# Feature halves of 288, token sums ahead of DMA transposes, and seven block products in more places

## The chip, the cores and the metric

The kernel runs on 1 core of one Trainium2 chip. The metric is device time in microseconds of the whole launch; lower is better. Engines are named as in the profile: PE (TensorE), DVE (VectorE), ACT (ScalarE), POOL (GpSimd), SP (the queue that issues most DMAs).

## The reference

With S = 2048 tokens, D = 576 features and a hidden width of 4608, all fp32:

```python
xn = layernorm(x)                                   # over the 576 features
a = xn @ dft_hid_re.T;  b = xn @ dft_hid_im.T       # first transform, 576 -> 2 x 576
A = dft_seq_re @ a - dft_seq_im @ b                 # last stage, over the 2048 tokens
B = relu(xn @ w1) @ w2                              # 576 -> 4608 -> 576
out = x + A + B
```

## The kernel before

*Precision.* Every fp32 operand is scaled by a power of two and split into a high and a low fp16 part (`split`: ACT writes the high part, DVE the low one). A product is three fp16 matmuls: high x high, high x low, low x high, summed in PSUM.

*Seven block products.* A block matrix product of 2x2 blocks is done with 7 instead of 8 block products, with sums of blocks made beforehand (the table `PRODUCTS`, names S1..S4 for sums of the left operand, T1..T4 for those of the right one).

*Blocks.* The hidden width is cut into 9 blocks of 512. For each block b and each of 4 groups g of 512 tokens (4 tiles of 128), the first layer makes h = relu(xn @ w1), and `mlp2` makes h @ w2 by seven products, one group behind. In blocks 0 and 1 the first layer is plain: `mlp1_group` and `mlp1_step` with 512-wide matmuls. From block 2 on `pair_products` does it by seven products of 256-wide matmuls, over halves of the features and of the group's tokens. The 576 features are 4 slices of 128 and a remainder of 64 rows, so four of the products carry the remainder in two extra matmuls (`REST`). The token sums that these products need are made in block 1 by `sums_x` on DVE and ACT, out of the already transposed xT.

*Start.* A tile of 128 tokens is loaded, `stats` and `normalize` make xn and its high part, `remainder` the low part (POOL, mostly), and `transposes` turns it on PE into PSUM, from where ACT copies it into xT. Block 0's output is summed in SBUF and stored to DRAM tiles (`spill`) at its end; later blocks add to `spill` by accumulating DMAs that POOL issues.

*End.* `dft1` multiplies each token tile by the hidden transform, four column quarters of 288 each, and writes operands R. After all 16 tiles the last stage runs over 16 units (p, kh), the two kh halves of a p one after the other, each of seven products of 24 matmuls; it adds to what is read back from `spill` and stores the output.

*Order.* The order of an engine's instructions is planned at compile time from a cost model and the order of the program; the kernel steers it by lists of steps (`todo`, `work`, `brief`) and by `issue_after`. DMA loads and stores go through SP, in order; accumulating ones through POOL.

Of the kernel before, what the change touches and what calls it, by code (L numbers as in the profile page):

```python
# [18 lines left out]
P = 128  # L19
S = 2048  # L20
D = 576
# [14 lines left out]
NKX = 2 * KM + 1  # L36

NW1 = 17  # L40
W1B = NW1 * P

BB = 2
# [6 lines left out]
def kernel(  # L50
# [29 lines left out]


    dbuf = dpool.tile([P, 4 * 5 * EH], F32, name="dbuf")
    dbufs = [dbuf[:, j * 5 * EH : (j + 1) * 5 * EH] for j in range(4)]


    accs = [accp.tile([P, TG, D], F32, name=f"acc{g}") for g in range(NG)]
    acc = [accs[t // TG][:, t % TG] for t in range(NT)]
# [14 lines left out]
    def load_w1(b, i, parts=1):  # L102
        pool, tag = (raw, "raw") if b else (mlp, "stage")
        r = raws["w1", b, i] = pool.tile([P, 2 * KT, P], F32, tag=tag, name=f"raw_w1_{b}_{i}")
        n = 2 * KT // parts
        for k in range(0, 2 * KT, n):
            nc.sync.dma_start(r[:, k : k + n], w1[b, i][:, k : k + n])
# [27 lines left out]
    idle = const.tile([P, P], F16, name="idle")  # L135
# [6 lines left out]
    colno, rowno = (const.tile([P, SQ], F32, name=n) for n in ("colno", "rowno"))  # L142
# [43 lines left out]
    xT = [xpool[g].tile([P, NKX + 1, G], F16, name=f"xT{g}") for g in range(NG)]  # L186
# [49 lines left out]

    def normalize(t, eng=nc.vector):
        stage = dbufs[t % 4]
        xn = xns[t] = stage[:, :D]

        xs = xss[t] = stage[:, D : 2 * D].bitcast(F16)
        eng.tensor_scalar(xn, acc[t], means[t], factors[t], ALU.subtract, ALU.mult)
        nc.scalar.activation(xs[:, :D], acc[t], AF.Identity, bias=shifts[t], scale=factors[t])

    def remainder(t, eng):
        xn, xs = xns[t], xss[t]
        eng.tensor_tensor(
            xs[:, D : D + REM], xn[:, KM * P :], xs[:, KM * P : D], ALU.subtract
        )
        eng.tensor_tensor(  # L250
            xs[:, D + REM :], xn[:, : KM * P], xs[:, : KM * P], ALU.subtract
        )

    def transposes(t):
        xs = xss[t]
        pt = ps2.tile([P, 2, 1024], F16, tag="ps2", name=f"pt{t}")
        for k in range(NKX):
            nc.tensor.transpose(
                pt[:, k // 8, (k % 8) * P : (k % 8 + 1) * P], xs[:, k * P : (k + 1) * P], ident
            )  # L260
        g, c = divmod(t, TG)

        nc.tensor.transpose(pt[:, 1, P : 2 * P], xs[:, D - P : D], ident)
        dst = xT[g][:, :, c * P : (c + 1) * P]
        nc.scalar.activation(
            dst[:, :8, :], pt[:, 0, :].rearrange("p (k t) -> p k t", t=P), AF.Copy
        )
        nc.scalar.activation(
            dst[:, 8:, :], pt[:, 1, : 2 * P].rearrange("p (k t) -> p k t", t=P), AF.Copy
        )  # L270

# [17 lines left out]
    XK = [(kx, hl, k) for k in range(KM) for kx, hl in ((k, 0), (k, 1), (KM + 1 + k, 0))]  # L298
    XK += [(KM, 0, KM), (KM, 1, KM)]
    WK = [(kx, hl, k) for k in range(KM) for kx, hl in ((k, 1), (k, 0), (KM + 1 + k, 0))]  # L300
    WK += [(KM, 0, KM), (KM, 1, KM)]

    WK0 = sorted(WK, key=lambda w: w[1])
    w1s, w2s, us, hs = {}, {}, {}, {}
    w1bufs = [mlp.tile([P, W1B], F32, name=f"w1buf{i}", bufs=1) for i in range(2)]
    w1bufs += [dbuf[:, i * W1B : (i + 1) * W1B] for i in range(2)]

    def mlp1_group(b, g, i, cols, ps, wk=WK, start=True, stop=True):
        for n, (kx, hl, k) in enumerate(wk):
            nc.tensor.matmul(  # L310
                ps[:, cols], w1s[b, i // 2][:, hl, i % 2 * KT + k], xT[g][:, kx, cols],
                start=(start and n == 0), stop=(stop and n == len(wk) - 1),
            )

    def new_ps1(b, g, i):
        return ps1.tile([P, G], F32, tag="ps1", name=f"p1_{b}_{g}_{i}")

    def mlp1(b, g, i):
        ps = new_ps1(b, g, i)
        mlp1_group(b, g, i, slice(0, G), ps)  # L320
        return ps

    def mlp1_step(b, g, i, ps):

        if i == 1:
            for j in range(NF):  # L330
                r, kx = j % 2, (KM, NKX)[j % 2]
                rows = slice(r * REM, (r + 1) * REM)
                if j:
                    ps.append(new_ps1(b, g, j))
                nc.tensor.matmul(
                    ps[j], w1s[b, j // 2][rows, 1, r * KT + KM], xT[g][rows, kx],
                    start=(j > 0), stop=(j == 0),
                )
        if i == 0:
            ps.append(new_ps1(b, g, 0))  # L340
        mlp1_group(b, g, i, slice(0, G), ps[i], WK[:-1], start=(i == 0), stop=(i > 0))

    def mlp1_out(b, g, i, pa, pb):
# [24 lines left out]
    LEFT = (0, 2, 8, 15, 13, 10, 5)  # L368
    REST = {P2: (4, 0), P5: (7, 1), P3: (12, 1), P4: (7, 0)}
    flat = [a.rearrange("p a b -> p (a b)") for a in accs]  # L370
    XS = 4 * 2 * (KM // 2) * GH // 2
    xsums = [
        f[:, : XS].bitcast(F16).rearrange("p (q n k t) -> p q n k t", q=4, n=2, t=GH)
        for f in flat
    ]
    cbufs = [f[:, XS :] for f in flat]
    H1, H2 = slice(0, GH), slice(GH, G)

    def halves(g, q):

        r, c = q
        k, t = 2 * r, (H1, H2)[c]
        return xT[g][:, k : k + 2, t], xT[g][:, KM + 1 + k : KM + 3 + k, t]

    def right(g, n):
        if n in (P1, P2, P3):
            return halves(g, {P1: (0, 0), P2: (1, 0), P3: (1, 1)}[n])
        x = xsums[g][:, {P5: 0, P6: 1, P4: 2, P7: 3}[n]]
        return x[:, 0], x[:, 1]

    def sums_x(g):


        f = [
            w[:, 2 * KT * P :][:, : 2 * GH].rearrange("p (k t) -> p k t", t=GH) for w in w1bufs[2:]
        ]
        tt = nc.vector.tensor_tensor
        for q, (head, tail) in enumerate((
            ((0, 1), (0, 0)), ((1, 1), None), ((1, 0), None), ((1, 1), (0, 1)),
        )):  # L400
            t = f[q % 2]
            h, l = halves(g, head)
            if tail:
                h2, l2 = halves(g, tail)
                tt(t, h, h2, ALU.subtract)
                tt(t, t, l2, ALU.subtract)
            else:
                tt(t, h, f[1 - q % 2], ALU.subtract)
            tt(t, t, l, ALU.add)
            yield  # L410
            hi, lo = (xsums[g][:, q, n] for n in range(2))
            nc.scalar.activation(hi, t, AF.Copy)
            yield
            tt(lo, t, hi, ALU.subtract)  # L414
# [7 lines left out]
    def pair_products(b, g, i):  # L422
# [10 lines left out]
        def product(n):  # L433
# [3 lines left out]
            todo = [  # L437
                (ws[:, y, a + k], x[z][:, k]) for k in range(2) for y, z in ((1, 0), (0, 0), (0, 1))
            ]
            if n in REST:  # L440
                k, c = REST[n]
                todo += [(ws[:, y, k], xT[g][:, KM, (H1, H2)[c]]) for y in range(2)]
# [51 lines left out]
    sumbufs = [mlp.tile([P, 2, EH], F32, name="sum0", bufs=1)] + [  # L494
        dbuf[:, k : k + 2 * EH].rearrange("p (c e) -> p c e", e=EH)
        for k in (2 * W1B, 2 * W1B + 2 * EH)
# [10 lines left out]
    def mlp2(b, g, n):  # L507
# [18 lines left out]
        blocks = accs[g].rearrange("p (h c) (j e) -> p h j c e", h=2, j=2)  # L526
        o = sums[row, col] = sums[row, col] if b else blocks[:, row, col]
        if b and n in (0, 2, 3, 6):
# [5 lines left out]
        if b and n not in (0, 2, 3):  # L534
            nc.gpsimd.dma_start(spill[g, row, col], o, accum_op=ALU.add)  # L535
        if b == 0 and n == 6:
            for r in range(2):
                for j in range(2):
                    nc.sync.dma_start(spill[g, r, j], blocks[:, r, j])
# [3 lines left out]
    def max_w1(b, f):  # L543
# [6 lines left out]
        with tc.issue_after(order["vfree"]) if b >= BB else nullcontext():  # L550
            magnitude(mx["f", b][:, r : r + 1], raws["w1", b, i][:, r * KT : (r + 1) * KT])
        if r:
            if b >= BB:
# [10 lines left out]
    def power_w1(b, i):  # L564
        s, p = (t["w1", b][:, i : i + 1] for t in (sc, pw))
        if b >= BB:
# [3 lines left out]

    def split_w1(b, f):
        i, r = divmod(f, 2)
        k = slice(r * KT, (r + 1) * KT)
        if r == 0:
            w = w1bufs[b % 2 * 2 + i].bitcast(F16)[:, : 4 * KT * P]
            w1s[b, i] = w.rearrange("p (n k f) -> p n k f", n=2, f=P)
        w = w1s[b, i]
        split(w[:, 0, k], w[:, 1, k], raws["w1", b, i][:, k], sc["w1", b][:, i : i + 1])

    def split_w1b(b, i, c):  # L580

        if c == 0:
            w = w1bufs[b % 2 * 2 + i].bitcast(F16)
            w1s[b, i] = w.rearrange("p (n k f) -> p n k f", n=2, f=P)
        w, r = w1s[b, i], raws["w1", b, i]
        src = (r[:, :5], r[:, 7:], r[:, :5], r[:, 5:9])[c]
        k = (slice(0, 5), slice(5, 8), slice(8, 13), slice(13, 17))[c]
        split(w[:, 0, k], w[:, 1, k], src, sc["w1", b][:, i : i + 1])

    def sums_w1(b, i):  # L590
        r = raws["w1", b, i]
# [632 lines left out]
```

## Time and profile before

| | |
|---|---|
| median of 2 runs | 1266.02 us (1264.86 to 1267.18) |
| span of the profiled execution | 1265.5 us; its page gives no other time |
| PE, DVE, ACT, POOL busy | 1242.4, 1024.9, 706.8, 148.9 us |
| mean granted PE clock | 0.995 |
| block 0 and 1 | 0 to 213 us |
| blocks 2 to 8 | 213 to 823 us |
| first transform | 823 to 929 us |
| last stage | 929 to 1262 us |

The boundaries are first and last starts of the matmul lines (310, 444, 1037, 1156). Busy time counts overlapping parts of an engine's pipeline once; the pace of matmuls is read from their starts.

### The profile page before, as it was taken

How to read it: one execution, taken by the hardware profiler on the slowest of the kernel's cores; microseconds unless marked ns; L12 is line 12 of the kernel's file. 1: busy time of each engine (PE TensorE's matmuls, PEld its weight loads, DVE VectorE, ACT ScalarE, POOL GpSimd, SP SyncE). 2: the span in 40 equal slices, each digit the busy share in tenths (PEclk: the TensorE clock that was granted, in tenths of full speed). 3: DMA queues.
4: the chain of work that ended last, by engine and by line, in shares of the span. 5: the costliest groups of instructions: out<-in, count | busy, mean ns of one | idle time of the engine just before them, and what ended most of it. 6: DMA issues, size and time to landing. Idle time of an engine off the chain costs nothing.

```text
span 1265.5 us, 25525 instructions
## 1 busy us (share of the span) xinstructions
PE 1242.4 (98%) x10396; PEld 991.3 (78%) x10396; DVE 1024.9 (81%) x1933; ACT 706.8 (56%) x1194; POOL 148.9 (12%) x188
## 2 busy tenths in 40 slices
PE   8899999999999999999999999999999999999998
PEld 7665566888888888888888888877777777777776
DVE  8899999778878787788798878556788888787875
ACT  5835466666676676676766766544453333333332
POOL 2320021121212121212121212100000000000000
PEclk8999999999999999999999999999999999999999
DMA  6022357666657676666666666630053434434320
GB/s 246 23 78 85 112 128 149 125 134 140 131 120 154 139 142 123 128 154 113 133 144 147 137 138 124 114 94 1 1 171 100 147 122 145 141 111 144 117 86 20
DMA packets 60806, 150.75 MB, mean 119 GB/s; under 512 B 6288, under 2 KB 21136, under 8 KB 60688
## 3 DMA queue, kind: packets, MB, share of 16 engines
q1 hardware_dynamic: 42256, 111.36, 26.8%
q0 software_dynamic: 18432, 37.76, 22.0%
q8 instruction: 81, 1.33, 0.4%
q14 instruction: 37, 0.30, 0.1%
HBM read 101.91 MB, written 47.19 MB: 118 GB/s over the span
## 4 chain that ended last, share of the span: by engine, by line
PE 79%; DVE 13%; ACT 3%; issue 2%; DMA 2%; SPq 0%; POOL 0%; ACTq 0%; DVEq 0%
PE p L521 24%; PE bank L444 23%; PE p L1156 22%; PE pd L1037 8%; DVE cs L183 1%; PE p L310 1%; DVE w2s L183 1%; DVE acc L532 1%; DMA raw_w<-in_w_dram 1%; DVE h L354 1%; DVE w1buf L183 1%; DVE acc L414 1%; DVE st L200 1%; DVE h L361 1%; DMA c<-in_cim_dram 1%
## 5 line engine op out<-in xcount | busy, mean ns | idle before, releaser
L521 PE MATMUL p<-w2s,h 128*128 128x288 f16 x3024 | 408.7, 286 | 3.1 <-DVE h L466 1.5
L521 PEld LDWEIGHTS <-h 128*128 128x128 f16 x3024 | 295.4, 98 | 78.2 <-issue 2.3
L1156 PE MATMUL p<-R,cs 128*128 128x288 f16 x2688 | 329.8, 286 | 2.5 <-DVE o L1162 2.5
L1156 PEld LDWEIGHTS <-cs 128*128 128x128 f16 x2688 | 263.0, 98 | 69.1 <-issue 2.9
L182 ACT ACTIVATE cs<-c,sc_c 128x1024 f16<-128x1024 f32 x112 | 128.0, 1147 | 195.0 <-PE p L1156 135.0
L183 DVE SCALAR_TENSOR_TENSOR cs<-c,sc_c,cs 128x1024 f16<-128x1024 f32 x112 | 143.4, 1283 | 40.6 <-ACT cs L182 40.5
L444 PEld LDWEIGHTS <-w1buf 128*128 128x128 f16 x1600 | 156.5, 98 | 23.0 <-issue 1.6
L444 PEld LDWEIGHTS <-dbuf 128*128 128x128 f16 x1200 | 117.4, 98 | 16.1
L444 PE MATMUL bank<-xT,w1buf 128*128 128x256 f16 x832 | 109.9, 273 | 0.0
L1037 PE MATMUL pd<-dbuf,xT 128*128 128x288 f16 x832 | 103.8, 286 | 0.0
L444 PE MATMUL bank<-acc,w1buf 128*128 128x256 f16 x768 | 102.1, 273 | 1.4 <-ACT acc L470 1.4
L1037 PEld LDWEIGHTS <-xT 128*128 128x128 f16 x832 | 80.8, 98 | 22.0 <-issue 1.9
L466 DVE TENSOR_TENSOR h<-s,h 128x1024 f16<-128x1024 f32 x56 | 68.5, 1224 | 33.9 <-ACT h L463 33.6
L451 ACT ACTIVATE h<-acc 128x256 f16<-128x256 f32 x112 | 46.0, 411 | 76.4 <-DVE acc L474 71.1
L535 POOL DMA_DIRECT2D spill<-dbuf x70 | 61.0, 876 | 232.9 <-DVE dbuf L532 194.2
L444 PE MATMUL bank<-xT,dbuf 128*128 128x256 f16 x624 | 82.5, 273 | 0.0
L463 ACT ACTIVATE h<-s 128x1024 f16<-128x1024 f32 x56 | 59.1, 1056 | 37.0 <-DVE s L458 36.4
L444 PE MATMUL bank<-acc,dbuf 128*128 128x256 f16 x576 | 76.6, 273 | 0.0
L1162 DVE SCALAR_TENSOR_TENSOR o<-p,us_c,o 128x288 f32<-128x288 f32 x112 | 57.5, 514 | 19.2 <-PE p L1156 19.1
L911 ACT ACTIVATE f<-f 128x1024 f32<-128x1024 f32 x64 | 66.9, 1046 | 0.8 <-DMA f<-in_cre_dram 0.8
L452 DVE SCALAR_TENSOR_TENSOR h<-acc,h 128x256 f16<-128x256 f32 x112 | 47.3, 422 | 21.1 <-ACT h L451 21.0
L530 ACT ACTIVATE dbuf<-p,c_ub 128x576 f32<-128x576 f32 x70 | 51.0, 730 | 15.3 <-PE p L521 15.0
(156 smaller groups left out, 1556.1 us busy)
## 6 DMA issues: line engine op xcount, KB each, us to landing
spill<-dbuf POOLq DMA_DIRECT2D x70, 288.0 KB, 5.3
f<-in_cre_dram SPq DMA_DIRECT2D x32, 512.0 KB, 5.9
f<-in_cim_dram SPq DMA_DIRECT2D x32, 512.0 KB, 5.6
c<-in_cre_dram SPq DMA_DIRECT2D x32, 512.0 KB, 4.2
c<-in_cim_dram SPq DMA_DIRECT2D x32, 512.0 KB, 4.7
spill<-sum POOLq DMA_DIRECT2D x42, 288.0 KB, 4.6
raw_w<-in_w_dram SPq DMA_DIRECT2D x17, 640.0 KB, 6.4
raw_w<-in_w_dram SPq DMA_DIRECT2D x18, 576.0 KB, 4.9
```

The costliest lines, as they stand in the source:

```text
L182: nc.scalar.activation(hi, src, AF.Copy, scale=s)
L183: nc.vector.scalar_tensor_tensor(lo, src, s, hi, ALU.mult, ALU.subtract)
L444: nc.tensor.matmul(ps, l, r, start=first and m == 0, stop=m == len(todo) - 1, skip_group_check=not first,)
L463: order["s"] = nc.scalar.activation(hi_s, st[:, 1:], AF.Copy).ins
L466: order["lo"] = nc.vector.tensor_tensor(lo_s, st[:, 1:], hi_s, ALU.subtract).ins
L521: nc.tensor.matmul(ps[:, c], h[:, x, qa, c * P : (c + 1) * P], w[:, y, qb], start=first and i == 0 and j == 0, stop=i == NQ - 1 and j == 2 ...
L530: freed(nc.scalar.activation(o, ps, AF.Copy, scale=us[b]))
L535: nc.gpsimd.dma_start(spill[g, row, col], o, accum_op=ALU.add)
L911: nc.scalar.activation(f, f, AF.Abs, scale=2.0**-10, accum_out=sums_c[:, n, q : q + 1])
L1037: nc.tensor.matmul(ps[j], xT[g][:, kx, c * P : (c + 1) * P], dsp[j][:, hl, k], start=(t % 2 == 0 and n == 0), stop=(t % 2 == 1 and n == le ...
L1156: nc.tensor.matmul(ps, w[:, a, k], r[:, c, rq], start=first and k == 0 and j == 0, stop=k == HK - 1 and j == 2, skip_group_check=not first,)
L1162: order["o"] = nc.vector.scalar_tensor_tensor(o, ps, us["c"][:, n : n + 1], o, ALU.mult, ALU.add).ins
```

## The change

*Feature halves.* The 576 features become two halves of 288, each with two slices of 128 and one packed slice: 32 remainder rows as high, high, low and zero. A half then needs 7 matmuls (`PASSES`): three for each full slice and one for the packed one. `load_w1` brings the remainder rows by broadcast DMAs (`load_rest`), `high`, `low` and `split_operands` build the packed slices.

*Transposes.* Tiles 0 to 3 stay on PE; tiles 4 to 15 are transposed by DMA from SP, SBUF to SBUF. The stages of the normalized tiles go from 4 to 7, and xn stays in the tile's own place.

*Token sums.* `sums_x` runs in block 0, on POOL, over the untransposed xn (four subtractions of blocks, each in two parts), splits the sums (ACT and POOL) and transposes them by DMA.

*Block 1* is done by `pair_products` too. Block 0 no longer sums in SBUF: `copy_x` copies x into `spill` from DRAM to DRAM, and block 0 adds to it like the others.

*First transform.* `dft1` is replaced by chains of seven products, over feature halves, token halves and column halves; the right sums of R are made afterwards on POOL or DVE. Half of its weights (`dsp[1]`) is prepared after block 8's first layer, in the place of block 8's weights.

*Last stage.* The order becomes: transform of token half 0, its 8 units (their results added to `spill` by POOL's DMAs), transform of half 1, its 8 units. Four of seven evictions per unit of half 0 go to ACT.

```diff
-    XK = [(kx, hl, k) for k in range(KM) for kx, hl in ((k, 0), (k, 1), (KM + 1 + k, 0))]
-    XK += [(KM, 0, KM), (KM, 1, KM)]
+    PASSES = [p for k in range(2) for p in ((3 + k, k), (k, k), (k, 3 + k))] + [(2, 2)]
...
     def transposes(t):
+        if t >= TG:
+            nc.sync.dma_start_transpose(dst, xs)
+            return
...
+    def load_rest(dst, src):
+        shape = list(src.shape)
+        nc.sync.dma_start(dst, src.unsqueeze(0).to_broadcast([P // RH] + shape))
...
     def sums_x(g):
+        b11, b21, b12, b22 = (half(pair(c), r) for c in range(2) for r in range(2))
+        for dst, a, b in ((b11, b12, b11), (b12, b22, b12), (b22, b22, b11), (b21, b21, b22)):
+            for k in range(2):
+                nc.gpsimd.tensor_tensor(dst[k], a[k], b[k], ALU.subtract)
+            yield
+        for c in range(TG):
+            st = spare[:, c % 2]
+            high(st, xns[t])
+            low(st, xns[t], nc.gpsimd)
+            if c < 2:
+                nc.sync.dma_start_transpose(s0[:, :, cols], st.rearrange("p r k c -> p (r k c)"))
+            else:
+                for r, dst in ((1, s1[:, :, cols]), (0, xT[g][:, :KC, GH:][:, :, cols])):
+                    nc.sync.dma_start_transpose(dst, st[:, r].rearrange("p k c -> p (k c)"))
+            yield
...
     def mlp2(b, g, n):
-        if b and n in (0, 2, 3, 6):
+        if n in (0, 2, 3, 6):
...
-        if b >= BB:
+        if b:
             first, second = (pair_products(b, g, i) for i in range(NQ))
...
+    load_later = prepare_d(1)
     for q in range(7):
         mlp2(*steps[-1], q)
+        for _ in range(2):
+            if load_later:
+                load_later.pop(0)()
...
+    def chain(g, c, z):
+        u, v, w = (bank(f"pd{t}_{z}_{k}") for k in range(3))
+        copy = lambda o, p: nc.scalar.activation(o, p, AF.Copy, scale=HALF)
+        add = lambda o, p: stt(o, p, HALF, o, ALU.mult, ALU.add)
+        def product(n):
+            ps = {P2: v, P5: w, P3: w}.get(n, u)
+            for m, (y, k) in enumerate(PASSES):
+                nc.tensor.matmul(ps, x[:, k, c * P : (c + 1) * P], dsp[z][:, a, y], ...)
+    def transform(kh, at):
+        for n, key in enumerate(keys + [None]):
+            for f, q in ((new, P1), (old, P7), (new, P2), (old, P3), (new, P6), (old, P4), (new, P5)):
...
+    transform(0, side)
+    for n in range(HK):
+        unit(n)
+    transform(1, side2)
+    for n in range(HK, 2 * HK):
+        unit(n)
```

More of the change, by code (lines that the diff above doesn't have):

```diff
@@ L79 @@
     ps2 = tc.alloc_tile_pool(name="ps2", bufs=2, space=PSUM)
[L82 to L87, printed above, removed]
+    dbuf = dpool.tile([P, 2 * W1B + 2 * SB + P], F32, name="dbuf")
+    wbuf = dpool.tile([P, 2 * W1B + SB], F32, name="wbuf")
+    NS = 7
+    stages = dbuf[:, : 2 * W1B].bitcast(F16).rearrange(
+        "p (n r k c) -> p n r k c", n=NS, r=2, k=KC
+    )
+    spare = wbuf[:, : 2 * W1B].rearrange("p (n w) -> p n w", n=2)[:, :, 4 * KC * P // 2 :]
+    spare = spare[:, :, : NX * P // 2].bitcast(F16).rearrange(
+        "p n (r k c) -> p n r k c", r=2, k=KC
+    )
+    accs = accp.tile([P, NG * XW], F32, name="accs")
+    last = [mlp.tile([P, 2, D], F32, tag="w2s", name=f"x{t}", bufs=4) for t in (NT - 4, NT - 2)]
+    acc = [accs[:, t * D : (t + 1) * D] for t in range(NT - TG)]
+    acc += [last[c // 2][:, c % 2] for c in range(TG)]
     spill = {
@@ L131, in power @@
         )
-    idle = const.tile([P, P], F16, name="idle")
+    idle = stages[:, NS - 1].rearrange("p r k c -> p (r k c)")[:, :P]
     nc.vector.memset(idle, 0.0)
@@ L318, in mlp1 @@
     def mlp1(b, g, i):
-        ps = new_ps1(b, g, i)
+        ps = ps1.tile([P, G], F32, tag="ps1", name=f"p1_{b}_{g}_{i}")
         mlp1_group(b, g, i, slice(0, G), ps)
         return ps
[L323 to L341, printed above, removed]
@@ L533, in mlp2 @@
             order["acc"] = order["vfree"] = add.ins
-        if b and n not in (0, 2, 3):
+        if n not in (0, 2, 3):
             nc.gpsimd.dma_start(spill[g, row, col], o, accum_op=ALU.add)
[L536 to L539, printed above, removed]
     sc, pw, mx = {}, {}, {}
@@ L792 @@
     qs = [pq[:, 0], pq[:, 1]]
-    T(5)
     tile_by(4, (0, 1), qs)
     mlp1_out(0, 0, 0, *ps[:2])
-    T(6)
     tile_by(5, (0, 1), qs)
-    T(7)
+    tq = itertools.chain(*(sums_x(g) for g in range(NG)))
     weave(stats([8, 9, 10, 11]))
@@ L821 @@
         mlp2(0, 0, q)
+    copy_x(1)
+    for _ in range(8):
+        next(tq)
     steps = [(b, g) for b in range(NB) for g in range(NG)]
@@ L916 @@
     passes.append(lambda: sum_c(4 * len(units) - 1))
-    tq = itertools.chain(*(sums_x(g) for g in range(NG)))
     for n in range(2, len(steps)):
@@ L963 @@
                 do(q)
-            for _ in range(4):
-                next(tq, None)
+            if 8 <= n < 16:
+                count(0)
             continue
@@ new lines, in run @@
+        def run(n):
+            product(n)
+            done(n)
+        return run
+    def transform(kh, at):
+        keys = [(g, c, z) for g in (2 * kh, 2 * kh + 1) for c in range(2) for z in range(2)]
+        old = None
+        for n, key in enumerate(keys + [None]):
+            new = chain(*key) if key else None
+            for f, q in (
+                (new, P1), (old, P7), (new, P2), (old, P3), (new, P6), (old, P4), (new, P5)
+            ):
+                if f:
+                    f(q)
+            old = new
+            at(n)
```

609 lines of the change are left out of this document (346 added, 263 removed).

## The prediction

> **What bounds the kernel now.** I read the page first: busy shares, slices, the chain that ended last.
>
> ```profile
> PE 1242.4 (98%) x10396; PEld 991.3 (78%) x10396; DVE 1024.9 (81%) x1933; ACT 706.8 (56%) x1194; POOL 148.9 (12%) x188
> PE   8899999999999999999999999999999999999998
> DVE  8899999778878787788798878556788888787875
> PE 79%; DVE 13%; ACT 3%; issue 2%; DMA 2%; SPq 0%; POOL 0%; ACTq 0%; DVEq 0%
> ```
>
> TensorE (PE) is busy everywhere and carries four fifths of the last chain. But a busy PE need not be a full one, so the next view is the table by stretches: block 0, steady blocks, the first transform, and the last stage at its start and further in.
>
> ```profile
> 30.00:40.00 10.00, 7.32 (x129) 7.02 (x126) 8.21 (x20) 7.89 (x16) 6.97 (x9) 1.00 0.01 2
> 50.00:60.00 10.00, 8.08 (x62) 4.70 (x61) 9.69 (x19) 10.00 (x18) 0.00 (x0) 1.00 0.03 4
> 300.00:385.00 85.00, 85.00 (x739) 72.12 (x738) 69.00 (x153) 57.59 (x115) 14.98 (x19) 1.00 0.64 136
> 823.00:929.00 106.00, 106.00 (x885) 82.00 (x884) 75.32 (x131) 51.36 (x82) 1.55 (x3) 1.00 0.11 29
> 929.00:1012.00 83.00, 80.52 (x657) 64.04 (x656) 68.03 (x78) 32.66 (x32) 0.00 (x0) 1.00 0.49 160
> 1012.00:1095.00 83.00, 83.00 (x680) 66.29 (x679) 67.72 (x74) 32.83 (x29) 0.00 (x0) 1.00 0.42 131
> ```
>
> The columns are busy us and counts of PE, PE weight load, DVE, ACT, POOL, then granted clock, DMA share and GB/s. From block 2 on PE never stops and has the full clock: there the time is the number of matmuls times their pace, and removing matmuls removes time. In block 0 PE has gaps while ACT or DVE is full: there the time is set by the feeding of PE. So the sum has two halves: PE work taken out, and waits moved.
>
> **PE work taken out.** The pace is the distance between starts in the timeline, since the busy time of a single matmul overlaps the next.
>
> ```profile
> 152.75 0.60 PE L335 MATMUL p<-xT,dbuf 64*128 64x512 f16 x4
> 153.29 2.98 PE L310 MATMUL p<-xT,dbuf 128*128 128x512 f16 x13
> 156.11 3.10 PE L521 MATMUL p<-w2s,h 128*128 128x288 f16 x24
> 159.05 2.97 PE L310 MATMUL p<-xT,dbuf 128*128 128x512 f16 x13
> 213.38 1.69 PE L444 MATMUL bank<-xT,w1buf 128*128 128x256 f16 x14
> 214.91 0.29 PE L521 MATMUL p<-w2s,h 128*128 128x288 f16 x1
> ```
>
> Thirteen 512-wide matmuls take 156.11-153.29 = 2.82 us; the four half-row ones 0.54; a 288-wide one (159.05-156.11)/24 = 0.1225; a 256-wide one 1.53/14 = 0.1093.
>
> *Block 1.* Per token group: 4 x 2.82 + 0.54 = 11.82 us of first-layer matmuls before. After: 2 halves x 7 products x 7 passes = 98 of 256 columns, 98 x 0.1093 = 10.71. Four groups save 4 x 1.11 = 4.4 us.
>
> *Blocks 2 to 8.* A half-block has 7 x 6 + 4 x 2 = 50 matmuls now and 49 after (each feature half carries its 32 remainder rows in one packed pass). 7 x 4 x 2 = 56 fewer, 56 x 0.1093 = 6.1 us.
>
> *First transform.*
>
> ```profile
> L1037 PE MATMUL pd<-dbuf,xT 128*128 128x288 f16 x832 | 103.8, 286 | 0.0
> L1047 PE MATMUL pd<-dbuf,xT 64*128 64x288 f16 x64 | 5.3, 285 | 0.0
> 828.19 0.67 PE L1047 MATMUL pd<-dbuf,xT 64*128 64x288 f16 x8
> 828.79 6.42 PE L1037 MATMUL pd<-dbuf,xT 128*128 128x288 f16 x51
> ```
>
> 832 x 0.1225 = 101.9, and 64 half-row ones at 0.60/8 = 0.075 make 4.8: 106.7 us, as the 106 us window says. After: 16 chains x 7 products x 7 passes = 784, 784 x 0.1225 = 96.0. Saved 10.7.
>
> *Transposes.*
>
> ```profile
> 94.10 0.66 PE L258 MATMUL pt<-ident,dbuf 128*128 128x128 f16 x9
> 94.60 0.22 PE L263 MATMUL pt<-ident,dbuf 128*128 128x128 f16 x1
> 94.65 0.90 PE L521 MATMUL p<-w2s,h 128*128 128x288 f16 x6
> ```
>
> Ten cost 0.55 us. Tiles 4 to 15 go by DMA: 12 x 0.55 = 6.6 us.
>
> The second layer (3024 matmuls) and the last stage (2688) keep their counts; the last stage only changes its order. Sum: 4.4 + 6.1 + 10.7 + 6.6 = 27.8 us.
>
> **Waits moved.**
>
> ```profile
> PE pt L258 <- ACT xT L268: 4.4, 4, 2.6
> PE p L310 <- ACT xT L265: 1.2, 2, 1.1
> PE p L521 <- ACT xT L268: 1.0, 1, 1.0
> ACT c L1057 <- DMA spill<-sums: 4.9, 1, 4.9
> ```
>
> *Gone with the PE transposes:* PE waited 4.4 + 1.2 + 1.0 = 6.6 us for ACT to empty transposed tiles. At most all of it goes, at least nothing (another input is then the last). ACT also loses 12 evictions, but gains a second, small instruction per tile and one split per sum tile, so it stays as full in block 0. I take 4 us off.
>
> *DMA transposes.* No row shows one. Each whole tile is 128 x 1280 of 2 bytes, 320 KB: 12 for the tiles, and per group two whole and four half ones for the token sums, 12 + 8 + 16/2 = 28 in all, every one issued on SP behind a POOL subtraction. The nearest rows:
>
> ```profile
> spill<-acc SPq DMA_DIRECT2D x16, 288.0 KB, 2.5
> acc<-in_x_dram SPq DMA_DIRECT2D x16, 288.0 KB, 7.0
> 29.60 1.38 POOL L250 TENSOR_TENSOR dbuf<-dbuf 128x512 f16<-128x512 f32 x1
> 59.22 0.46 ACT L268 ACTIVATE xT<-pt 128x256 f16<-128x256 f16 x1
> 191.23 2.97 PE L310 MATMUL p<-xT,dbuf 128*128 128x512 f16 x13
> ```
>
> Between 2.5 us (a quiet queue) and 7.0 us (eight loads at once). Tile 4's remainder ends at 31.0; tiles 4 to 11 must lie in xT by 59.7 to be as early as now: eight in series have 28.7/8 = 3.6 us each. All 28 must be through before block 1's last group, which begins at 191 now and, less 6.6, 4 and three groups of 1.1, at some 177 then: (177-31)/28 = 5.2 us each. I take the lower row, because SBUF to SBUF in block 0 competes with little (DMA share 0.01 and 0.03 above): then they cost nothing, hidden behind the matmuls of groups 0 and 1. If that cover is gone, group 1 waits first.
> [...]
>
> *Token sums on POOL.* DVE loses 5 instructions per sum (lines 405 to 414) and half of block 0's evictions. POOL gains 64 subtractions, half of them long. What they do to DVE:
>
> ```profile
> 27.22 0.15 DVE L218 TENSOR_SCALAR u<-u 128x4 f32<-128x4 f32 x1
> 34.06 1.09 DVE L218 TENSOR_SCALAR u<-u 128x4 f32<-128x4 f32 x1
> ```
>
> The same instruction takes 0.94 us more while POOL subtracts. 32 long ones x 0.94 = 30 us of DVE at most, 0 at least, in a stretch where DVE is full. The relief is of like size, so I take +2 us of PE.
>
> *Weights.* Each half-block's split handles 2688 instead of 2176 elements, and its sums 1536 instead of 1152:
>
> ```profile
> L183 DVE SCALAR_TENSOR_TENSOR w1buf<-raw_w,c_sw,w1buf 128x640 f16<-128x640 f32 x20 | 17.9, 900 | 2.3 <-ACT w1buf L182 2.2
> 207.11 0.33 SPq L107 DMA_DIRECT2D raw_w<-in_w_dram  x1
> 226.38 0.81 DVE L115 TENSOR_REDUCE c_mf<-raw_w 128x1 f32<-128x640 f32 x1
> ```
>
> At 1.4 ns per element 900 more elements are 1.3 us, 2.6 per block of 85 us with DVE at 69: hidden behind PE; without that cover, 8 x 2.6 = 21 us. The weight load becomes three DMAs, two of them broadcasts of 32 rows; it is used 19 us after its issue, so nothing is late. At the start there is no such lead (the first reduction waits for it): +1 us, 0 to 3.
>
> *Into the transform.* Its first eviction waits for the last spill to land:
>
> ```profile
> 822.59 5.68 PE L1037 MATMUL pd<-dbuf,xT 128*128 128x288 f16 x45
> 829.50 0.50 ACT L1057 ACTIVATE c<-pd,c_rho 128x288 f32<-128x288 f32 x1 [4.93 <-DMA spill<-sums]
> ```
>
> Now PE has 6.9 us of matmuls in eight banks that need no eviction, and loses nothing. After, a chain's third product adds to a bank that ACT must first have copied, and the new tiles (tb, R) lie where the spill reads. Independent are P1, P2, P5 and the next chain's P1: four products of 7 x 0.1225 = 0.86. So 6.9 - 3.4 = 3.5 us of stall, between 0 (other addresses, other order) and 6.9. The second half of the transform weights is split only after block 8's last first-layer product; its 12 DVE and 12 ACT steps of 0.5 to 0.8 us have the last second-layer step (84 x 0.1225 = 10.3 us) plus 3.4 us as cover: just enough, 0, at most 4. Take +3.5.
>
> *Last stage.* The first window lacked 2.5 us of PE; twice such a start costs 0 to 2.5 more, I take +1. The added spills per unit, 8 x 4, go on POOL, which is idle there; the four ACT copies per unit (ACT is busy 33 of 83) relieve DVE (68 of 83).
>
> Sum: 1265.5 - 27.8 - 4 + 2 + 1 + 3.5 + 1 = 1241.2 with waits at my values. The two windows of block 0 shown lack 2.7 and 1.9 us of PE, only in part the waits named; with ACT relieved of evictions at 10.00 of 10 I take half of it, another 2.3. Forecast: 1238.9, rounded **1239 us**. The median of the runs, 1266.02, is 0.5 above the profile's span, which is inside the rounding.
>
> **Rivals.**
> *A. Waits eat most of it (about 1250).* Bounds at their upper ends: spill 6.9 instead of 3.5, split weights 4, DVE under POOL 6 instead of 2: 3.4 + 4 + 4 = 11.4. For it: DVE at 9.7 and more in block 0, and evictions now stand inside each chain (ACT copy 0.5 us, then PE). Against: a chain leaves three products, 2.6 us, for each copy.
> *B. Slow DMA transposes (1289 or more), slower than before.* At 7.0 us each in series they end at 31 + 28 x 7 = 227, where block 1's last group wants them at 177: +50, and more where the early groups can't fill the time with other matmuls. It decides from 5.2 us each, and the kernel is slower than before from about 5.2 + 27/28 = 6.2. For it: series on one queue, each behind POOL. Against: the 2.5 us row. [...]
> *C. Block 0 gets shorter (about 1226).* PE's idle time at 30 to 110 us goes almost wholly, since DVE and ACT are relieved and the transform starts without stall: 9 more from block 0, 3.5 from the spill. Against: POOL under DVE.
>
> **Chances.** Forecast 0.47 (own range 1231 to 1247), A 0.25, B 0.12, C 0.16. A measurement of this kernel tells about 2% from no change, 1240.7 us: faster holds C and some 0.31 of the forecast, 0.47; slower is the part of B above 1291, 0.09; the rest, 0.44, is the same. The range that leaves out 2 in 10 is 1224 to 1262: it takes in A and most of C.
>
> **What would show it.** Right: 3136 matmuls of 256 columns, 784 in the transform at 0.1225, PE full from block 1 on, DMA transposes landing within 3.6 us. Step wrong: PE waiting for a DMA of xT in 35 to 110 us (B); DVE instructions stretched beside POOL, or ACT copies of the chains as PE's releaser (A); a steady block not 0.9 us shorter (8 x 0.1093). A pace of the transform above 0.125 would contradict its term.

## The result, and the profile after

The changed kernel takes 1396.01 us (median; 1391.68 to 1400.34), the kernel before 1266.02: a ratio of 1.102 (95% interval 1.094 to 1.111). The forecast was 1239 us; 157 us lie between. The changed kernel was run only twice, with 8.7 us between the two, so each difference to it below is sure to some 4 us only. The page of the profiled execution (span 1389.9 us), its busy shares, its slices of PE and of the granted clock, and the chain that ended last:

```profile
PE 1257.0 (90%) x10276; PEld 1004.6 (72%) x10276; DVE 1050.7 (76%) x1925; ACT 759.5 (55%) x1350; POOL 307.3 (22%) x378
PE   6776899988899999999999997869799999899998
PEclk8978999999999999999999999989899999999999
PE 40%; DVE 25%; DMA 13%; ACT 9%; issue 7%; POOL 4%; SPq 2%; POOLq 0%; ACTq 0%; DVEq 0%
```

PE, at 8 or 9 tenths in every slice before, has gaps in three places: the first quarter, two thirds along (the entry to the transform) and near the end. PE's share of the chain falls from 79% to 40%, and DMA, 2% before, has 13%. The table by stretches (columns as in the prediction) shows the first layer of block 0, then blocks 2, 3 and 5, each about as long as one block:

```profile
16.90:157.60 140.70, 98.98 (x763) 65.67 (x762) 110.75 (x219) 73.76 (x136) 84.83 (x103) 0.85 0.78 165
250.50:343.00 92.50, 82.93 (x688) 68.55 (x686) 67.67 (x151) 57.84 (x116) 13.35 (x18) 0.96 0.64 141
343.00:436.00 93.00, 82.37 (x685) 68.10 (x683) 68.70 (x148) 59.09 (x116) 14.99 (x19) 0.96 0.65 144
529.00:622.00 93.00, 91.28 (x786) 76.61 (x785) 80.67 (x175) 62.62 (x122) 15.90 (x20) 1.00 0.61 128
```

In 140.7 us of block 0 PE works 99.0 at 0.85 of its clock, while DMA, at 0.25 in the like stretch before (11.6 to 128 us), is at 0.78. Blocks 2 and 3 lack 10 us of PE each and some of the clock. The waits of PE over the whole span (total, times, longest) are spread over many causes:

```profile
PE bank L478 <- ACT s L506: 23.4, 10, 3.6
PE pd L1120 <- ACT tb L1109: 16.4, 11, 4.7
PE p L361 <- DMA xT<-dbuf: 11.6, 2, 7.5
PE p L555 <- ACT sums L563: 10.1, 4, 5.6
```

Before, none was above 4.4. So no single wait explains 157 us; the experiments take the causes one by one. Each had the kernel before beside it on its chip (1266.2 to 1267.4 us).

### The profile page after: what moved, and what is told of

The parts are those of the page before. It is cut to its first block, busy times and chain, and to the rows that moved or that the text cites. A ratio compares the mean times of both kernels' runs of the same rounds, so it can differ in the third digit from the quotient of the medians.

```text
span 1389.9 us, 25975 instructions
## 1 busy us (share of the span) xinstructions
PE 1257.0 (90%) x10276; PEld 1004.6 (72%) x10276; DVE 1050.7 (76%) x1925; ACT 759.5 (55%) x1350; POOL 307.3 (22%) x378
## 4 chain that ended last, share of the span: by engine, by line
PE 40%; DVE 25%; DMA 13%; ACT 9%; issue 7%; POOL 4%; SPq 2%; POOLq 0%; ACTq 0%; DVEq 0%
PE p L1241 16%; PE p L555 12%; PE bank L478 10%; DVE R L1090 3%; DMA raw_w<-in_w_dram 2%; DMA f<-in_cre_dram 2%; PE pd L1120 2%; DVE h L500 2%; DMA f<-in_cim_dram 2%; DVE cs L223 2%; DMA raw_dk<-in_dft_dram 2%; ACT R L1089 1%; ACT f L965 1%; DVE h L486 1%; DVE dbuf L609 1%
## 5 line engine op out<-in xcount | busy, mean ns | idle before, releaser
L555 PE MATMUL p<-w2s,h 128*128 128x288 f16 x3024 | 426.3, 293 | 30.7 <-ACT sums L563 10.1
L478 PEld LDWEIGHTS <-wbuf 128*128 128x128 f16 x1568 | 155.1, 99 | 45.3 <-issue 22.8
L478 PE MATMUL bank<-xT,wbuf 128*128 128x256 f16 x896 | 114.4, 277 | 12.5 <-ACT s L506 12.5
L222 ACT ACTIVATE cs<-tb,sc_c 128x1024 f16<-128x1024 f32 x56 | 63.5, 1146 | 87.3 <-PE p L1241 59.8
L485 ACT ACTIVATE h<-accs 128x256 f16<-128x256 f32 x128 | 52.0, 412 | 105.0 <-DVE accs L508 79.8
L478 PE MATMUL bank<-accs,wbuf 128*128 128x256 f16 x672 | 87.3, 274 | 7.5 <-DVE accs L508 7.1
L223 DVE SCALAR_TENSOR_TENSOR cs<-tb,sc_c,cs 128x1024 f16<-128x1024 f32 x56 | 71.6, 1281 | 26.7 <-ACT cs L222 26.4
L478 PE MATMUL bank<-accs,dbuf 128*128 128x256 f16 x672 | 86.4, 272 | 3.2 <-DVE accs L508 2.8
L361 PE MATMUL p<-xT,wbuf 128*128 128x128 f16 (+1 forms) x476 | 59.7, 290 | 20.9 <-DMA xT<-dbuf 11.6
L1090 DVE TENSOR_TENSOR R<-tb,R 128x288 f16<-128x288 f32 (+1 forms) x64 | 52.2, 840 | 31.4 <-ACT R L1089 30.8
L222 ACT ACTIVATE cs<-accs,sc_c 128x1024 f16<-128x1024 f32 x40 | 45.6, 1146 | 51.8 <-PE p L1241 28.8
```

Source lines behind the costliest of these rows:

```text
L222: nc.scalar.activation(hi, src, AF.Copy, scale=s)
L223: nc.vector.scalar_tensor_tensor(lo, src, s, hi, ALU.mult, ALU.subtract)
L361: nc.tensor.matmul(ps[:, cols], w1s[b, i // 2][:, i % 2 * 2 + h, y], xT[g][:, h * KC + z, cols], start=(n == 0), stop=(n == len(wk) - 1),)
L478: nc.tensor.matmul(ps, l, r, start=first and m == 0, stop=m == len(todo) - 1, skip_group_check=not first,)
L555: nc.tensor.matmul(ps[:, c], h[:, x, qa, c * P : (c + 1) * P], w[:, y, qb], start=first and i == 0 and j == 0, stop=i == NQ - 1 and j == 2 ...
L1090: order["lo"] = tt(lo, src, hi, ALU.subtract).ins
```

## The experiments

### A line outside the sum: the third sweep pass

A part of the change that the prediction never priced: the sweep that sums the magnitudes of the last stage's operands (`passes`: load f, reduce it on ACT, two per step of a block) starts two steps later, and runs a third time at the end of each step of blocks 2 and 3. The timeline there:

```profile
327.78 0.82 PE L478 MATMUL bank<-xT,wbuf 128*128 128x256 f16 x6
330.10 1.06 ACT L965 ACTIVATE f<-f 128x1024 f32<-128x1024 f32 x1 [3.64 <-DMA f<-in_cre_dram]
331.78 0.37 ACT L506 ACTIVATE s<-bank 128x256 f32<-128x256 f32 x1
332.20 1.08 PE L478 MATMUL bank<-xT,wbuf 128*128 128x256 f16 x7 [3.60 <-ACT s L506]
```

There is one buffer f. The extra pass follows the last one so closely that its load is under way; ACT stands 3.64 us for it, the copy that frees PE's bank (L506) comes behind, and PE stands 3.60.

```diff
-            count = lambda q: n > 5 and passes and passes.pop(0)()
+            count = lambda q: n > 3 and passes and passes.pop(0)()
...
-            if 8 <= n < 16:
-                count(0)
```

> Edit to the changed kernel: the third magnitude pass over the sequence matrices in each step of blocks 2 and 3 is taken out, and the two passes per step begin in block 1 instead, as in the kernel before. Theory A (the third pass comes so soon after the second that ACT waits for its load, about 3 us, nine times seen in the trace, and PE with it): 1396 falls by 27 to 35 us to 1361 to 1369, and blocks 2 and 3 run as fast as blocks 4 to 7. Rival (ACT's waits only fill time that something else, late weights, would take): less than 10 us, and the same windows stay slow with another releaser.

Measured: 1363.01 (1360.52 to 1363.11), ratio 1.076 [1.074, 1.077], 33.0 us less, as theory A said. PE in block 2 is full again:

```profile
251.00:338.00 87.00, 86.67 (x754) 73.45 (x752) 75.34 (x165) 60.21 (x121) 16.14 (x21) 1.00 0.68 139
```

The other way round, the same extra pass was put alone into the kernel before.

> The kernel before with one line of the change: the third sweep pass in each step of blocks 2 and 3. Theory A (the pass finds its only buffer's load under way, ScalarE stands for it, and TensorE's banks are freed late, whatever else is changed): 18 to 33 us slower than before, 1284 to 1299 us. Rival B (the kernel before has slack enough for it, and the pass only costs together with the other parts): within 6 us of 1266.

Measured: 1300.09 (1297.40 to 1300.96), ratio 1.026 [1.023, 1.028]: 32.7 us slower than the 1267.4 beside it, as theory A said. The waits in blocks 2 and 3 of that run are of the same kind:

```profile
ACT f L911 <- DMA f<-in_cre_dram: 13.4, 5, 3.3
PE bank L444 <- ACT s L472: 15.0, 6, 3.5
```

The cost stands for itself and needs no other part of the change. It is larger than these waits; one reason is the granted clock, 0.989 over the profiled execution of that run, where the kernel before beside it has 0.994 to 0.999 (for the stages see the last section).

### Repeated remainder rows

In the next run the remainder rows lie packed for 128 partitions in DRAM, so that one contiguous load, in place of three, brings a half block; the broadcasts go, for the transform's weights too.

```diff
-                    load_rest(r[:, :, 2]..., src[h * RH : (h + 1) * RH, :, KM])
+            nc.sync.dma_start(r[:, f[0] : f[1]], w1[b, i][:, f[0] : f[1]])
...
-        load_rest(r[:, 2 * f + h], dft[h * RH : (h + 1) * RH, KM, e])
+        nc.sync.dma_start(r[:, 2 * f + h], dftr[:, h, e])
```

> Edit to the changed kernel: the packed remainder rows of w1 and of the hidden transform lie in DRAM as the kernel wants them, so each weight load is one contiguous transfer and nothing is broadcast from 32 rows. Theory B (the broadcasts are slow and hold up what is queued with them: the first reduction began at 9.7 us against 5.2 before, and ACT waited 7.6 us for a slice of transform weights at 914 us): 15 to 30 us less, 1366 to 1381, with the first reduction back at 5 to 6 us and no wait at the entry of the transform. Rival (the loads are late because the whole DMA system is full): under 8 us.

Measured: 1382.56 (1381.12 to 1395.87), ratio 1.094 [1.089, 1.099], 13.4 us less, between the two theories. Its slowest run lies inside the changed kernel's range, so the gain is better read from the run with both edits below. The start gains (the first reduction of the weights, in the changed kernel and in this run):

```profile
9.74 0.95 DVE L580 TENSOR_REDUCE c_mf<-raw_w 128x1 f32<-128x768 f32 x1 [3.96 <-DMA raw_w<-in_w_dram]
```

```profile
6.42 0.95 DVE L569 TENSOR_REDUCE c_mf<-raw_w 128x1 f32<-128x768 f32 x1 [0.55 <-DMA raw_w<-in_w_dram]
```

The other sign that theory A named did not come: at the entry to the transform ACT still waits for a load of its weights, 4.51 us instead of 7.59, and 8.1 in the run with both edits below.

In the first 20 us the DMA engines moved 215 GB/s on the mean in the changed kernel, 341 in this run and 339 in the kernel before. The edit takes the broadcasts away and also makes three loads one; which of the two gains is not shown.

Both edits together:

> Both earlier edits together: the third sweep's extra passes of blocks 2 and 3 are taken out, and the remainder rows of the weights lie packed in DRAM, so that no load repeats them. Theory A (the two losses lie in different stages, blocks 2 to 8 and the start with the entry to the transform): they add, 1396 - 33 - 13.4 = 1350 us, between 1344 and 1356. Rival B (what the start gains is taken back by the next wait for block 0's transposes or by the extra passes' clock): 1357 to 1363, no better than the first edit alone.

Measured: 1347.73 (1346.73 to 1352.03), ratio 1.065 [1.063, 1.067], 48.3 us less, where the single ones add to 46.4. The packed rows are worth 15.3 here (1363.01 to 1347.73), with ranges well apart. What follows builds on this run.

### The transposes by DMA, rival B of the prediction

```diff
-        if t >= TG:
-            nc.sync.dma_start_transpose(dst, xs)
-            return
```

> Edit to the changed kernel: tiles 4 to 15 are transposed on PE again, only the token sums go by DMA. Theory C (the DMA transposes of tiles are what blocks 0 and 1 wait for; PE waited 16 us for xT from a DMA): 15 to 25 us less. Rival (the transposes run at some 2 us each and only wait for their input, which comes late from DVE and POOL): between 5 us less and 8 us more, the 6.6 us of PE work and the evictions being back.

Measured: 1411.34 (1410.67 to 1412.17), ratio 1.115 [1.113, 1.116]: 15.3 us slower than the changed kernel, more than either theory allowed. Undoing them costs; they are not what is slow. The same was done again at the end, with all other known costs gone ("the run with the six costs taken out" below, 1282.29):

> As the run with the six costs taken out, and tiles 4 to 15 are transposed on TensorE as in the kernel before. Theory A (with the token sums gone, what still keeps block 0 late is the wait for transposes by DMA, some 10 us): 3 to 8 us below that run, since TensorE takes 6.6 us of work back. Rival B (the transposes by DMA cost nothing that TensorE's own would not): 4 to 8 us above it.

Measured: 1295.98 (1291.78 to 1296.84), 13.7 us slower again, outside both expectations. Nearly all of it lies before block 2, which starts at 224.2 instead of 211.3. The first layer of block 0, in this run and in the one it starts from:

```profile
13.00:132.90 119.90, 98.29 (x882) 66.43 (x882) 89.74 (x217) 75.94 (x127) 34.15 (x43) 0.97 0.21 77
```

```profile
12.80:120.00 107.20, 91.08 (x762) 62.74 (x762) 90.49 (x216) 61.60 (x103) 35.30 (x42) 0.92 0.47 121
```

Of the 12.7 us, 7.2 are PE's own work on 120 transposes and 5.5 are more idle time. ACT has 14 us more to do. PE's waits with the transposes on PE:

```profile
PE pt L307 <- POOL dbuf L290: 5.3, 7, 1.2
PE pt L307 <- ACT dbuf L281: 5.2, 6, 1.5
PE pt L307 <- POOL dbuf L289: 2.2, 5, 1.1
```

A transpose on PE stands in PE's order, and the matmuls behind it wait while POOL and ACT finish the tile: 12.7 us, where with transposes by DMA PE waits 10.1 for xT. By DMA the wait for the tile lies on SP (in the first 160 us of the run with the six costs taken out):

```profile
SPq L306 <- ACT dbuf L284: 29.5, 2, 15.5
SPq L306 <- POOL dbuf L290: 13.9, 8, 5.1
```

The transfers themselves (from the issues of the 1332.66 us run below; the last column is the median of us from issue to landing) are slower than the prediction's 2.5 us, and the 24 for the token sums, 16 of which the prediction counted as halves, are no faster than whole tiles:

```profile
xT<-dbuf SPq DMA_TRANSPOSE x12, 3.6
accs<-wbuf SPq DMA_TRANSPOSE x16, 4.1
xT<-wbuf SPq DMA_TRANSPOSE x8, 4.7
```

### Token sums and copies in block 0

> Edit to the changed kernel: the token sums and the low parts of their splits run on DVE instead of POOL. Theory D (POOL's subtractions hold up the remainders of the tiles that PE waits for, and stretch DVE's instructions beside them): 10 to 25 us less. Rival (DVE was full in block 0 before, so the work is no cheaper there): within 6 us, or slower.

The edit puts the eight subtractions of `sums_x` and the sums' `low` on `nc.vector`. Measured: 1395.26 (1390.68 to 1400.51): no change, as the rival said. Block 0's first layer ends 21 us sooner (136.6 instead of 157.6), but block 1 takes 16 longer (first starts 136.8 and 243.6 of blocks 1 and 2, instead of 159.6 and 250.6), with 92.1 us of DVE work in it instead of 78.5: DVE gives most of it back. The rest is lost in blocks 2 to 8, with the third pass still in them; why, this run doesn't settle. The order alone, with both edits above:

```diff
+                with tc.issue_after(order["rem"]):   # the newest tile's remainder
                     nc.gpsimd.tensor_tensor(dst[k], a[k], b[k], ALU.subtract)
```

> As the run with both edits, and the token sums on GpSimd may only be issued behind the newest token tile's remainder, so that no token sum of an early group stands ahead of a tile that the first layer of block 0 still waits for. Theory A (block 0 is set by tiles that wait behind token sums on GpSimd and behind their transfers): 8 to 20 us below the run with both edits, block 2 starts 8 to 20 us sooner. Rival B (GpSimd and VectorE have too much work in this stretch whatever its order): within 5 us of it; block 0 ends sooner and block 1 later by as much.

Measured: 1344.80 (1341.32 to 1347.98), 2.9 us below the run with both edits: rival B. Its sign came too: block 0's first layer ends at 144.2 instead of 152.4, and block 2 starts at 245.3, where it started at 245.0. So it is the amount, and the next two runs take it away. They build on the 1332.66 us run of the next section.

> As the run with packed rows, without the extra passes and with the transform's left sums on VectorE (1333 us), and all work for the token sums is left out (the GpSimd subtractions, the splitting and their 16-bit transfers; the sums are zeros, so this part of the result is missing; TensorE does the same products). Theory A (the token sums, put into block 0, are what keeps blocks 0 and 1 some 42 us over their TensorE work): block 2 starts 20 to 35 us sooner, 1298 to 1313 us. Rival B (block 0 waits for statistics, normalization and loads, and the sums fill gaps): block 2 starts at most 8 us sooner, 1325 to 1333 us.

> As the run without token sums, and the copies of x into the spill are left out too (block 0 writes its spill plainly, so x is missing from the sum). Theory A (the copies lie beside other transfers and nobody waits): within 4 us of the run without token sums. Rival B (the copies hold up the loads and transposes of block 0, whose transfers take 0.7 to 0.8 of the DMA engines' time): 8 to 15 us below it.

Measured: 1303.63 (1301.99 to 1305.85), 29.0 us less, as theory A said, and 1298.46 (1296.15 to 1299.16), another 5.2 less, between the two theories for the copies (block 0's stores, plain in that run instead of accumulating, are part of the 5.2). The first layer of block 0 with the sums and without them:

```profile
12.60:155.90 143.30, 104.72 (x776) 68.29 (x776) 108.12 (x218) 73.59 (x136) 87.49 (x105) 0.82 0.75 159
```

```profile
12.80:124.50 111.70, 91.23 (x762) 62.24 (x762) 90.44 (x216) 61.80 (x103) 37.62 (x42) 0.91 0.70 158
```

POOL has 50 us less to do, ACT 12, and DVE, with 218 and 216 instructions, 18: DVE's work took longer beside POOL's subtractions. The same two sums of weights on DVE (count, busy us, mean ns), beside those subtractions and without them, show it:

```profile
L668 DVE TENSOR_TENSOR raw_w<-raw_w 128x288 f32<-128x288 f32 x2 | 2.7, 1372 | 0.0
```

```profile
L652 DVE TENSOR_TENSOR raw_w<-raw_w 128x288 f32<-128x288 f32 x2 | 0.9, 449 | 0.0
```

The run leaves out the subtractions, their splits and their transposes together, so what each of them costs is not shown.

### Sums on GpSimd around the transform

The entry of the changed kernel in the timeline: block 8's last second-layer matmuls, ACT splitting the transform's weights between them, and the first chains.

```profile
914.68 0.78 ACT L925 ACTIVATE wbuf<-raw_dk,c_sdm 128x576 f16<-128x576 f32 x1 [7.59 <-DMA raw_dk<-in_dft_dram]
916.13 6.41 PE L555 MATMUL p<-w2s,h 128*128 128x288 f16 x36 [5.60 <-ACT sums L563]
919.66 0.80 POOL L629 TENSOR_TENSOR raw_dk<-raw_dk 128x288 f32<-128x288 f32 x1
920.49 0.78 ACT L925 ACTIVATE wbuf<-raw_dk,c_sdm 128x576 f16<-128x576 f32 x1 [1.70 <-POOL raw_dk L629]
922.38 0.78 PE L1120 MATMUL pd<-dbuf,accs 128*128 128x288 f16 x5
926.19 1.02 PE L1120 MATMUL pd<-wbuf,accs 128*128 128x288 f16 x7
927.05 0.90 PE L1120 MATMUL pd<-dbuf,xT 128*128 128x288 f16 x6
932.14 1.32 ACT L1109 ACTIVATE tb<-pd 128x288 f32<-128x288 f32 x4 [7.93 <-DMA spill<-sums]
932.60 1.84 PE L1120 MATMUL pd<-dbuf,accs 128*128 128x288 f16 x7 [4.65 <-ACT tb L1109]
```

ACT waits for the load of the weights, then for their sums on POOL (L628 to L631), and the last spill's landing (7.93) holds the first chains. Three edits: the left sums (which changes their engine and their place at once), the place of the buffers that wait for the spill, and the right sums, which follow in every chain:

```diff
-            left_sums(*(r[:, q] for q in range(4)), nc.gpsimd)    # of the transform's weights
+            left_sums(*(r[:, q] for q in range(4)), nc.vector)    # one step sooner
...
+    for t in (1, 3, 4, 5, 6, 7):       # buffers R ahead of tb
+        new_r(t)
...
-        eng = nc.gpsimd if t % HK < HK - 3 else nc.vector
+        eng = nc.vector
```

> As the run with both edits, and the left sums of the transform's weights are taken on VectorE one step sooner, where GpSimd made them just before ScalarE reads them. Theory A (ScalarE stands for them, and the first layers of the last block stand behind ScalarE): 4 to 10 us below the run with both edits, all of it in the last block and the entry to the transform. Rival B (what the entry waits for is the spill's landing, and the sums are hidden by that): within 3 us.

> As the run with both edits, and the transform's buffers are allotted in another order, so that its first two products write where sums of an early group lay and not where the last spill is still being read. Theory A (the entry waits for the last spill's landing because its first buffer lies on it): 4 to 8 us below the run with both edits, the 7.9 us wait of ScalarE for the spill gone. Rival B (the wait moves to the next buffer that lies there, or the transform's weights are late by as much): within 3 us.

> As the 1333 us run, and the right sums of the transformed tokens are all taken on VectorE (288 numbers: about 0.46 us each) in place of GpSimd (0.8 to 0.95 us each). Theory A (the chain from the last product of a tile through these sums and the splitting to ScalarE's next eviction sets the pace of the two transforms, 12 and 9 us over their TensorE work): 6 to 14 us below. Rival B (the chain is ScalarE's and VectorE's own work, and VectorE gets more of it): within 3 us of it, or slower.

Measured: left sums 1332.66 (1331.47 to 1337.30), 15.1 us below the run with both edits, more than expected. In the profiles 8.6 of it lie in block 8, where the first half of the weights is prepared (759.9 to 858.3, then 761.1 to 850.9), and 7.4 between its first layer and the transform (to 882.0, then 867.2). The buffers in another order 1347.04 (1344.95 to 1349.24), nothing (ACT still waits 5.8 us for the spill). The right sums, on top of the left ones, 1317.50 (1313.58 to 1319.52), 15.2 us below, a little more than expected. The right sums in the first transform of the 1332.66 us run and of this one (busy us, mean ns):

```profile
L1082 POOL TENSOR_TENSOR tb<-tb 128x288 f32<-128x288 f32 x24 | 22.8, 952 | 27.1 <-PE pd L1107 10.2 <-ACT tb L1096 9.1 <-DVE R L1077 7.1
```

```profile
L1082 DVE TENSOR_TENSOR tb<-tb 128x288 f32<-128x288 f32 x24 | 10.5, 455 | 0.6
```

952 ns on POOL are 455 on DVE, four in a row in each chain. All edits that keep the whole computation:

> All edits that kept the whole computation and did not cost time, together: no extra passes, packed rows, the transform's left sums and right sums on VectorE, token sums behind the newest tile's remainder, the transform's buffers in the other order. By theory A the savings of the right sums (6 to 14) and of the order (3) add to the 1333 us run: 1316 to 1324 us, still some 50 us over the kernel before. Rival B (right sums on VectorE save nothing): 1327 to 1332 us.

Measured: 1316.71 (1313.25 to 1320.66), ratio 1.040 [1.037, 1.042]: inside theory A's range, but the same as 1317.50, so order and buffers add nothing to it. No version with the whole computation beats the kernel before.

### The six costs at once

> All six known costs taken out at once: no extra passes, packed rows, the transform's left and right sums on VectorE, and (these two parts of the result are missing) no token sums and no copies of x. Theory A (the costs lie in different stages and add): 1317.5 - 29 - 5 = 1283 us, between 1279 and 1289, still 17 us over the kernel before, although TensorE has some 27 us less to do. Rival B (they cover for each other): below 1275, or above 1293.

Measured: 1282.29 (1278.27 to 1284.26), ratio 1.012 [1.009, 1.014]. The costs add, as theory A said, because they lie in different stages. The profiled executions, in us (first start of block 2's first layer; from there to the last second-layer matmul of block 8; the rest of the span):

| run | block 2 starts | blocks 2 to 8 | rest |
|---|---|---|---|
| kernel before | 213.4 | 609.1 | 443.0 |
| changed kernel | 250.6 | 671.7 | 467.6 |
| without the third pass | 251.3 | 643.7 | 466.2 |
| and packed rows | 245.0 | 637.0 | 463.0 |
| and left sums on DVE | 246.7 | 620.5 | 463.6 |
| and no token sums | 217.2 | 621.6 | 463.1 |
| and no copies of x | 212.1 | 622.4 | 462.7 |
| and right sums on DVE: all six | 211.3 | 618.9 | 446.3 |

From the first and last starts of its matmul lines (the middle figures are durations; "211.3" is the start of block 2, "830.2" the end of block 8) and some of its waits of PE:

```profile
L451 PE MATMUL bank<-xT,wbuf x896: 272/273/273, 211.3 to 812.9; 128*128 128x256 f16 x180
L528 PE MATMUL p<-w2s,h x3024: 282/286/297, 62.2 to 830.2; 128*128 128x288 f16 x189
PE p L350 <- DMA xT<-dbuf: 10.1, 3, 6.2
PE bank L451 <- DVE accs L481: 5.6, 9, 1.6
PE 1223.7 (96%) x10276; PEld 992.0 (78%) x10276; DVE 1043.6 (82%) x1997; ACT 748.2 (59%) x1318; POOL 190.0 (15%) x246
```

## Why the prediction was wrong

Six causes explain some 114 of the 157 us: third pass 33.0, token sums 29.0, right sums 15.2, left sums 15.1, repeated rows 13.4, copies of x 5.2 add to 110.9, and the run without all of them lies 113.7 below the changed kernel. By the prediction's own steps:

- **PE work taken out (-27.8).** It held as far as it can be seen: a product of the transform takes (927.05 - 926.19)/7 = 0.123 us per matmul as forecast, and PE is busy 1223.7 us instead of 1242.4 in the last run, 18.7 less, though clock drops (0.92 in block 0's first layer) stay in that figure. The step that failed is to take this off the span, with the feeding of PE at +2, +1 and +3.5 or at nothing. "PE full from block 1 on" did not come, and the three signs that the prediction named for a wrong step all came: PE waits for xT, ACT's copies in the chains release PE (16.4 us), and a steady block is not 0.9 us shorter (last paragraph).
- **DMA transposes (0 at 2.5 us each, rival B from 5.2).** The value was low: the tiles of block 0 took 3.6 us (median, 1332.66 us run) to land, just the limit named, and those for the token sums 4.1 and 4.7; the 2.5 us was the row of a plain store, and no run shows it as the median of a transpose. PE waits 11.6 us for the tiles in the changed kernel and 10.1 in the last run. But with the transposes on PE the time was 14 to 15 more. That the time lies beyond rival B's 1289 is luck: it had the right sign and the wrong cause.
- **Token sums on POOL (+2).** 29 us: the most mis-sized term. The prediction saw that DVE is stretched (0 to 30 us; it was 18) and set the relief of DVE against it. The sums' own work, 50 us on POOL, 12 on ACT and 24 transposes, in a stretch where the feeding of PE sets the time, had no price. Another order (2.9) or engine (0.8) did not remove it; which part of the work costs most stays open.
- **Weights ("nothing is late", +1).** The repeated rows cost 13 to 15; by the table 6.3 of it lie before block 2, 6.7 in blocks 2 to 8 and 3.2 behind them. The left sums of the transform's weights cost 15: some 7 where the prediction had "0, at most 4" for the split, and 8.6 in block 8, for which it had nothing. It counted steps of DVE and ACT, and not the four subtractions on POOL, 0.8 us each, that ACT waits for, nor the load.
- **Into the transform (+3.5).** The wait for the spill is there (PE 4.65 in the timeline). Another order of the buffers doesn't remove it.
- **Not in the sum.** The third pass (33, in the change but not in the prediction's list), the right sums (15; they stand between a chain and ACT's next eviction) and the copies of x (5).

What remains above the forecast in the last run's profile (span 1276.5, so 37.6 over 1238.9) is placed by its rows. Block 2 starts at 211.3, where the prediction's terms give 199.1 (213.4 - 4.4 - 6.6 - 4 + 2 + 1 - 2.3): 12.2. Of these, 4.4 are block 1, which takes 89.3 us as before (122.0 to 211.3, 124.1 to 213.4) although its matmuls need 4.4 less at their pace; the others lie ahead of it, where PE waits 10.1 for xT. Blocks 2 to 8 take 618.9 instead of 609.1 - 6.1: 15.9. PE's listed waits there add to 13.7, 9.9 for DVE and 3.8 for ACT, against 2.9 before. Block 2, with little wait, takes 84.5 us (first starts 211.3 and 295.7), but blocks 2 to 7 take 86.1 on the mean (to 727.9), where 85.5 before (213.4 to 726.2) less 0.9 were due. So the pace held and the feeding did not: the prediction hid 2.6 us of added DVE work per block behind PE, and that cover was not enough. The rest takes 446.3 where 436.8 was due: 9.5. PE's listed waits there are 12.5 against 2.5 before, where the prediction added 4.5; 5.1 of them are ACT's copies in the chains. All of this paragraph is read from the profile, not tested.

## What to carry to other kernels

Read a diff for each instruction whose place or count changes, also a line that no headline names: the costliest one here was two lines in a loop, with one buffer and a DMA behind it. When PE is full, work removed from PE is worth its time only if every engine that feeds it finishes sooner too (the run with the six costs taken out has PE busy 18.7 us less and a ratio of 1.012); sum the added work by engine and stretch (here POOL and DVE in block 0) before taking it off. An engine that is nearly idle over the span is no free place for an operation that the next step waits for (here the right sums on POOL, 15.2 us).

## What the runs showed of the hardware

- **Two stalls of PE cost more than their own length.** In the changed kernel, after 5.60 us without work, 36 matmuls of 288 take 922.38 - 916.13 = 6.25 us, where 36 x 0.1225 = 4.41 was the pace: 1.84 more. The granted clock (the third figure from the end) is 0.50 from 917 to 919 us and 1.00 from 920 to 922:

```profile
917.00:919.00 2.00, 2.00 (x11) 1.25 (x9) 0.51 (x1) 1.16 (x2) 0.21 (x1) 0.50 0.02 7
920.00:922.00 2.00, 2.00 (x18) 1.60 (x17) 1.15 (x2) 0.78 (x1) 1.84 (x3) 1.00 0.01 4
```

In blocks 2 and 3 of that kernel, with waits of up to 3.6 us for ACT's copies, it is 0.96, and 1.00 where the third pass is gone. In the run with packed rows alone, after a stall of 2.52 us, the same 36 matmuls take 927.14 - 921.06 = 6.08 us, 1.67 more than at the pace, with 0.50 from 922 to 924 us:

```profile
921.06 6.24 PE L544 MATMUL p<-w2s,h 128*128 128x288 f16 x36 [2.52 <-ACT sums L552]
927.14 0.78 PE L1109 MATMUL pd<-dbuf,accs 128*128 128x288 f16 x5
922.00:924.00 2.00, 2.00 (x10) 1.29 (x9) 0.45 (x2) 0.31 (x2) 1.64 (x3) 0.50 0.00 0
```

- **The same subtraction of 288 numbers took 952 ns on POOL (1332.66 us run) and 455 on DVE (1317.50 us run)**, on the mean of 24, in the same place of the same chain.
- **DVE's subtractions took longer beside POOL's.** A subtraction of 288 numbers on DVE took 1372 ns on the mean beside the token sums on POOL, and 449 in the same place without them (rows in the section on token sums). In the changed kernel the eight such sums of weights in block 0 took 918 to 1465 ns, and those from block 2 on 442 to 451.
